# Idle transposes in the early gaps of a planned kernel, five places for raw weights, and a new order of its steps

## The chip, the cores and the metric

The kernel runs on one core of a Trainium2 chip. The metric is the device time of one execution in microseconds (us); lower is better. The engines are TensorE (PE for its matmuls, PEld for its weight loads), VectorE (DVE), ScalarE (ACT), GpSimd (POOL) and SyncE (SP, which here issues nearly all DMA transfers).

## What is computed

A banded attention with four sink keys feeds a gated MLP whose gate is a short convolution along the sequence. There are 4 batches, 8 heads, 768 positions and a head size of 64; the MLP is 512 wide with 1024 hidden units.

```python
scores = scale * np.matmul(q, k.transpose(0, 1, 3, 2))
keep = (pos[None, :] < n_sink) | ((rel >= 0) & (rel < window))     # n_sink 4, window 128
a = softmax(np.where(keep, scores, -1e9))
x = (a @ v) as (B, S, H * D)
h = np.maximum(x @ w_in, 0.0)
conv_out = sum(conv_w[k] * shifted(h, k) for k in range(3))
out = (h * sigmoid(conv_out)) @ w_out
```

The inputs q, k and v are 32-bit floats; `w_in`, `conv_w` and `w_out` come as 64-bit floats and are narrowed on the core.

## The kernel before

**Work.** The attention goes by pairs of heads (`g`, 16 of them, four in a batch) and by query tiles of 128 rows (`t`, six in a pair). For a tile, `scores` multiplies the queries with up to two tiles of keys, VectorE masks and takes the row maximum, ScalarE takes the exponential and its sum, GpSimd divides; `transp` transposes the probabilities on TensorE and GpSimd cuts them into two triangles; `pv` multiplies three tiles with v. Pairs 0 to 3 (batch 0) multiply in plain 32 bits, and their matmuls use 64 rows of the array (`narrow="rows"`); the later ones split each operand into a high and a low part. `pv` writes 64 columns of the array (`narrow=True`). The result goes to `x`, in two parts.

The MLP goes by units: 96 of them, each 128 hidden columns of 256 positions. A unit has twelve matmuls into one bank of PSUM (`ph`, line 791), a gate on ScalarE, VectorE and GpSimd, and twice three matmuls into the accumulators `po` (line 827). The units of a batch can begin when its four pairs have written `x`.

**Weights.** Seventeen pieces of raw weights (eight of `w_in`, eight of `w_out`, the taps) are read by SP at line 718 into places in `room[1]`, the space that later holds `x` of batch 1. There are three places. ScalarE and VectorE narrow each piece (lines 650 and 728 to 731), ScalarE rounds the high part, and GpSimd (for `w_in`) or VectorE (for `w_out`, line 744) takes the low part. A place is free when the narrowing has read it. `room[0]` holds a stretch of zeros in its first 792 columns.

**Order.** The kernel's order is not that of the program's loops. Every step is declared with an engine, an assumed duration, what it reads and writes, and a priority `at`, made from the numbers in `LAY`. `Plan.run` walks through time: for each engine it takes, among the steps whose inputs are ready (or will be within `SLACK`), the one of the lowest priority; a buffer is a `Place` with a number of slots (`PLACES`), and a step waits for a slot. TensorE's steps are assumed to take twice as long while the plan holds its clock to be low. The order that comes out is what is issued, engine by engine; on the chip each engine then works through its list in order. Two `po` banks are lent to the scores until these have taken `LENT` (36) slots, two for a tile.

**Start and end.** Before the branch on `n_sink` and `window`, TensorE does 13, 3 and 4 transposes of the identity into an unused tile (line 1271 and 1275), with the first transposes of q and k between them; the first halves of q and k are loaded by SP (line 345). At the end the two last output tiles are copied out of PSUM, the first by ScalarE with its store on ScalarE's queue, the second whole by VectorE (line 833) with its store on SP's.

Of the kernel before, what the change touches and what calls it, by code (L numbers as in the profile page):

```python
# [17 lines left out]
P = 128  # L18
# [10 lines left out]
RAWB = 4  # L29
# [310 lines left out]
def load(c, g, nm, t, lo, hi):  # L340

    b, hp = divmod(g, c.H // 2)
    for j in range(2):
        src = getattr(c, nm)[b, 2 * hp + j].rearrange("(t p) d -> p t d", p=P)
        c.nc.sync.dma_start(t[:, :, j, :], src[:, lo:hi])
    return t


def load_half(c, g, nm, half, slot):
    n = c.S // P // 2  # L350
    return load(c, g, nm, slot, n * half, n * half + n)
# [10 lines left out]
SLACK = {"PE": 0, "ACT": 0, "DVE": 21, "POOL": 451, "SP": 0}  # L362
SWITCH = 95
WINDOW, SHIFT = 3413.0, 0.0
# [3 lines left out]
CONV, GATED, PICK, WIL = "sbuf", False, 0, "POOL"  # L368
CARE = 112.0
LENT = 36  # L370
# [63 lines left out]
class Plan:  # L434
# [39 lines left out]
    def run(self):  # L474
        free = dict.fromkeys(("PE", "ACT", "DVE", "POOL", "SP"), 0.0)
        slow, window, used, kind = True, SHIFT, 0.0, None
# [22 lines left out]
        while left:  # L499
# [13 lines left out]
            e = o.eng  # L513
            if e == "PE" and o.narrow != mode:
                t += SWITCH + (70 if mode else 0)
                mode = o.narrow
# [3 lines left out]
            if e == "PE":  # L520
                while t >= window + WINDOW:
                    slow = used < (0.97 if slow else 0.55) * WINDOW
                    window, used = window + WINDOW, 0.0
                if slow:
                    busy, late = 2.0 * busy, late + busy
                used += busy
# [25 lines left out]
            if o.size:  # L552
                fabric = max(t + o.busy, fabric) + o.size / 225.0
                o.end = fabric + 1150.0
# [20 lines left out]
        return order  # L575


class Banded:


    def __init__(self, c):
# [26 lines left out]
        self.raws = [self.room[1][:, 1024 * i:1024 * i + 1024] for i in range(3)]  # L608
        self.zero = self.nc.gpsimd.to_reg(0.0)
        self.tiles = 0  # L610

# [51 lines left out]
    def dma(self, size, fn, r, w, n=1, busy=500, **kw):  # L663
        return self.p.op("SP", busy * n, busy * n, fn, r, w, size=size, **kw)
# [3 lines left out]
    def setup(self):  # L668
        c, nc, p = self.c, self.nc, self.p
        p.at = -9.0  # L670
        p.op("DVE", 1900, 1900, lambda: None, (), ("before", "tri", "m0", "m1", "m2"))
        p.op("POOL", 200, 200, lambda: None, (), ("vs",))
        p.at = LAY["zeros"]
        self.pool(760, lambda: nc.gpsimd.memset(self.zeros, 0.0), ("room",), ("zeros",), port=False)
# [36 lines left out]
    def weight(self, name, src, at, taps=None, parts=None, spot=None, engine=None, early=1.5):  # L711
# [6 lines left out]
        self.dma(rows * n * (8 if wide else 4), lambda: nc.sync.dma_start(dst() if not wide else dst().bitcast(I32), src if not wide else src.bitcast(I32)), ("room",), (raw,), busy=410)  # L718
        p.at = at
        if wide:  # L720
            low = self.turn("st", [P, 512], F32, f"{name}l")
            w = self.turn("st" if CONV == "sbuf" else "h", [P, 512], F32, f"{name}w")
# [3 lines left out]
            two = CONV == "sbuf"  # L726
            self.act(lv, lambda: f(words(1)), n + 60, (raw, "room"), (low,), scale=2.0 ** -112, sbuf=True)
            self.dve(n, lambda: nc.vector.tensor_scalar(wint(), lint(), 3, None, ALU.logical_shift_left), (low,), (w,), fast=two, port=two)
            self.dve(n, lambda: nc.vector.scalar_tensor_tensor(out=wint(), in0=words(0), scalar=29, in1=wint(), op0=ALU.logical_shift_right, op1=ALU.bitwise_or), (raw, w, "room"), (w,), port=two)
            v, vv = (low, lv) if not two and (taps is not None or engine == "POOL") else (w, wv)  # L730
            self.dve(n, lambda: nc.vector.scalar_tensor_tensor(out=vv().bitcast(I32), in0=lint(), scalar=-0x80000000, in1=wint(), op0=ALU.bitwise_and, op1=ALU.bitwise_or), (low, w), (v,), port=two)
            w, wv = v, vv
# [9 lines left out]
        psum = wide and CONV != "sbuf" and engine != "POOL"  # L742
        self.act(lambda: H, wv, n, (w,), ((name, "H"),), sbuf=not psum)
# [493 lines left out]
def attention_gated_mlp(ctx: ExitStack, tc: tile.TileContext, q, k, v, n_sink, window, w_in, conv_w, w_out, out):  # L1237
# [7 lines left out]
    with tc.manual_schedule():  # L1245
# [14 lines left out]
        for i in range(2):  # L1260
            load_half(c, 0, "qk"[i], 0, c.raw[i])
# [86 lines left out]
```

## Time and profile before

| what | us |
| --- | --- |
| median of 3 runs | 469.26 |
| lowest and highest | 467.88, 469.94 |
| the profiled execution's own time | 469.77 |
| its span, first to last instruction | 468.0 |
| TensorE busy in the span | 444.2 |
| VectorE, ScalarE, GpSimd busy | 358.2, 323.6, 295.8 |

The profile is one execution. The time around the span is 1.77 us. "Busy" of TensorE counts from the start of a matmul to its modelled end, so neighbouring matmuls overlap. The granted clock is a share of full speed. In a list of waits, the engine and line that waited stand first, then what ended the wait, the sum in us, the number and the longest. In a timeline a row is a run of like instructions: its start, its length, the engine, line, operation, output and inputs, the number, and in brackets the idle time before it.

### The profile page before, as it was taken

Reading aid. Unit: us, or ns where it says so; the run is one execution under the profiler, and the core shown is the slowest. Engines: PE = TensorE matmul, PEld = TensorE weight load, DVE = VectorE, ACT = ScalarE, POOL = GpSimd, SP = SyncE. Lnnn points to the kernel's source line nnn. Section 1 sums busy time; section 2 is a strip of 40 time slices with the busy share of each in tenths; the row PEclk is TensorE's granted clock in tenths of the full one; section 3 lists DMA queues with packets and bytes.
Section 4 is the critical chain, followed back from the end, with each engine's and each line's share of the span. In section 5 each row is a group of like instructions: output and inputs, shape, how many; then the busy total and the mean of one; then the engine's idle time right before and its main releaser. Section 6 shows DMA issues by size and latency. Waiting matters only on the chain.

```text
span 468.0 us, 10388 instructions
## 1 busy us (share of the span) xinstructions
PE 444.2 (95%) x3097; PEld 377.4 (81%) x3097; DVE 358.2 (77%) x1260; ACT 323.6 (69%) x1054; POOL 295.8 (63%) x587
## 2 busy tenths in 40 slices
PE   7678879999999999999999999999999999999995
PEld 6445657778888887988898988888898888999883
DVE  6788999999889987796777787697876764555552
ACT  3998877878788887775777786686775753545451
POOL 3698787767867777646565776657577672444442
PEclk9999989999999999999999999999999999999999
DMA  6797797415252433060513224160210010101011
GB/s 149 208 245 185 217 265 198 93 33 128 75 114 49 112 107 80 18 147 24 131 52 86 53 75 109 23 166 1 56 61 0 9 40 0 46 1 47 1 46 53
DMA packets 87306, 41.01 MB, mean 88 GB/s; under 512 B 80160, under 2 KB 80184, under 8 KB 87240
## 3 DMA queue, kind: packets, MB, share of 16 engines
q1 hardware_dynamic: 86952, 39.99, 33.5%
q8 instruction: 27, 0.44, 0.4%
q14 instruction: 39, 0.32, 0.2%
q10 hardware_dynamic: 288, 0.26, 0.2%
HBM read 27.60 MB, written 6.29 MB: 72 GB/s over the span
## 4 chain that ended last, share of the span: by engine, by line
PE 81%; DMA 8%; DVE 4%; ACT 3%; issue 1%; POOL 1%; SPq 1%; ACTq 0%; DVEq 0%
PE ph L791 29%; PE po L827 28%; PE px L1080 7%; DMA roomL<-in_moe_w_in_dram 4%; PE sc L983 4%; PE pts L1022 4%; PE sc L984 3%; PE tk L910 2%; PE tq L932 2%; PE px L1088 1%; DMA raw<-in_k_dram 1%; ACT pe L995 1%; DMA sc_i<-in_window_dram 1%; DMA roomL<-in_moe_conv_w_dram 1%; DMA vsr<-roomH 1%
## 5 line engine op out<-in xcount | busy, mean ns | idle before, releaser
L827 PE MATMUL po<-woH,g 128*128 128x512 f32 x384 | 149.0, 405 | 0.0
L1001 POOL TENSOR_SCALAR pe<-pe,sm 128x132 f32<-128x132 f32 (+1 forms) x192 | 90.1, 480 | 52.5 <-DVE sm L999 35.4
L791 PE MATMUL ph<-xH,wiL 128*128 128x258 f32 (+1 forms) x384 | 111.1, 293 | 0.0
L791 PE MATMUL ph<-xH,wiH 128*128 128x258 f32 (+1 forms) x384 | 109.2, 288 | 0.9 <-DVE kk L916 0.5
L791 PE MATMUL ph<-xL,wiH 128*128 128x258 f32 (+1 forms) x384 | 109.4, 289 | 0.0
L995 ACT ACTIVATE pe<-pe,sm 128x132 f32<-128x132 f32 (+1 forms) x192 | 76.9, 402 | 19.9 <-DVE sm L990 19.3
L816 POOL TENSOR_SCALAR g<-t 128x256 fp32r<-128x256 f32 x96 | 43.1, 449 | 63.6 <-DVE t L815 42.9
L827 PEld LDWEIGHTS po<-woH,g 128*128 128x128 f32 x384 | 72.4, 189 | 10.2
L817 POOL TENSOR_TENSOR g<-t,g 128x256 fp32r<-128x256 f32 x96 | 76.2, 794 | 6.8
L791 PEld LDWEIGHTS ph<-xL,wiH 128*128 128x128 f32 x384 | 72.1, 189 | 5.7 <-issue 2.6
L791 PEld LDWEIGHTS ph<-xH,wiH 128*128 128x128 f32 x384 | 72.1, 189 | 5.5 <-ACT pe L995 0.9
L827 PE MATMUL po<-woL,g 128*128 128x512 f32 x192 | 75.8, 395 | 0.0
L791 PEld LDWEIGHTS ph<-xH,wiL 128*128 128x128 f32 x384 | 72.2, 190 | 4.1 <-issue 2.5
L812 DVE SCALAR_TENSOR_TENSOR t<-hb,cw,t 128x256 f32<-128x256 f32 x96 | 53.5, 558 | 25.8 <-ACT t L650 25.6
L815 DVE SCALAR_TENSOR_TENSOR t<-t,hb 128x256 f32<-128x256 f32 x96 | 44.3, 465 | 24.9 <-ACT t L646 24.5
L646 ACT ACTIVATE t<-t 128x256 f32<-128x256 f32 x96 | 40.0, 420 | 32.2 <-DVE t L813 31.8
L1032 POOL TENSOR_SCALAR_AFFINE_SELECT pT<-pT 128x256 f32<-128x256 f32 x80 | 38.2, 478 | 32.8 <-ACT pT L648 28.4
L646 ACT ACTIVATE hb<-ph 128x258 f32<-128x258 f32 (+1 forms) x96 | 36.9, 385 | 29.4 <-PE ph L791 27.4
L650 ACT ACTIVATE t<-hb,cw 128x256 f32<-128x256 f32 x96 | 49.0, 512 | 11.2 <-POOL g L817 8.0
L813 DVE SCALAR_TENSOR_TENSOR t<-hb,cw,t 128x256 f32<-128x256 f32 x96 | 52.6, 549 | 1.9
L990 DVE CUSTOM_DVE_ANT_0 pe<-sc,m 128x132 f32<-128x132 f32 (+1 forms) x192 | 51.0, 287 | 4.0 <-PE sc L984 2.4
L989 DVE COPY_PREDICATED sc<-before,sc 128x128 f32<-128x128 int32 x160 | 43.0, 289 | 12.7 <-PE sc L984 10.1
(182 smaller groups left out, 860.6 us busy)
## 6 DMA issues: line engine op xcount, KB each, us to landing
raw<-in_q_dram SPq DMA_DIRECT2D x64, 96.0 KB
raw<-in_k_dram SPq DMA_DIRECT2D x64, 96.0 KB
out_dram<-out SPq DMA_DIRECT2D x23, 256.0 KB
kk<-kk SPq DMA_DIRECT2D x24, 198.0 KB
vraw<-in_v_dram SPq DMA_DIRECT2D x24, 192.0 KB
roomL<-in_moe_w_in_dram SPq DMA_DIRECT2D x8, 512.0 KB
roomL<-in_moe_w_out_dram SPq DMA_DIRECT2D x8, 512.0 KB
vraw<-in_v_dram SPq DMA_DIRECT2D x8, 128.0 KB
```

Of the source, the lines that this page charges most:

```text
L646: nc.scalar.activation(o, i, func, **({} if scale is None else {"scale": scale}))
L650: nc.scalar.mul(o, i, scale() if callable(scale) else scale)
L791: nc.tensor.matmul(h.ap[:, 0:W], self.wi[i][:, cc, ff * P:(ff + 1) * P], x[k][:, cc, t0:t1], start=(q == 0), stop=(q == len(prods) - 1))
L812: self.dve(324, lambda: stt(out=uv(), in0=this(), scalar=cw(1), in1=yv(), op0=ALU.mult, op1=ALU.add), (hb, y), (u,), port=not gated)
L813: self.dve(324, lambda: stt(out=yv(), in0=nxt(), scalar=cw(2), in1=uv(), op0=ALU.mult, op1=ALU.add), (hb, u), (y,), port=not gated)
L815: self.dve(256, lambda: stt(out=a.ap, in0=uv(), scalar=1.0, in1=this(), op0=ALU.add, op1=ALU.mult), (u, hb), (a,), port=not gated)
L816: self.pool(355, lambda: nc.gpsimd.tensor_scalar(g.ap[:, 0], a.ap, 1.0, 1.0, ALU.mult, ALU.mult), (a,), ((g, 0),))
L817: self.pool(685, lambda: nc.gpsimd.tensor_tensor(out=g.ap[:, 1], in0=a.ap, in1=f(g.ap[:, 0]), op=ALU.subtract), (a, (g, 0)), ((g, 1),), po ...
L827: nc.tensor.matmul(po.ap[:, 0:c.DM], g.ap[:, k, tt * P:(tt + 1) * P], w[:, ff, :], start=(ff == 0 and i == 0), stop=(ff == NFF - 1 and i = ...
L990: self.dve(n + 14, lambda pc=pc, j=j: nc.vector.tensor_tensor_reduce(out=pe()[:, j, cols], in0=pc.ap[:, P:SW][:, cols], in1=mk, op0=ALU.ad ...
L995: p.op("ACT", 395, 505, lambda j=j: nc.scalar.activation(pe()[:, j, cols], pe()[:, j, cols], AF.Exp, bias=sm[:, j:j + 1], scale=-1.0, accu ...
L1001: work = (lambda e, j=j: e.tensor_scalar(pe()[:, j, cols], pe()[:, j, cols], sm[:, 8 + j:9 + j], 1.0, ALU.mult, ALU.mult), ((smk, 8), (pt, ...
```

## The change

- **Idle transposes.** When the plan takes a TensorE step before `WARM` (75 us of plan time) that also takes a PSUM bank (`h`, `sc`, `pts` or `px`), and TensorE would stand idle before it, the plan puts `n` transposes of the identity in front, into that bank: as many as fill `FILL` (0.9) of the gap at 110 ns each. They wait for the bank to be released, as the step does.
- **Places.** Raw weights get five places instead of three; the two new ones are columns 1024 to 3071 of `room[0]`. The raw halves of q and k get five instead of four (`RAWB`).
- **Plan.** The model of a changing clock goes; assumed rates of transfers by kind, `LAND`, `ROWS`, `SLACK`, `CARE` and nearly all priorities in `LAY` are new; `LENT` is 48 instead of 36.
- **Start.** The first half of k is loaded from ScalarE's queue. The mask `tri` is no longer made (nothing used it). The zeros of `room[0]` have another priority and follow the masks.
- **End.** The next to last output tile is stored by SP; the last one is copied in two halves at once, by VectorE and by ScalarE, each with its own store, on SP's and ScalarE's queue (`close`).
- Options that were off (`GATED`, `PICK`, `CONV`, `WIL`) are taken out without an effect.

```diff
-RAWB = 4
+RAWB = 5
...
-SLACK = {"PE": 0, "ACT": 0, "DVE": 21, "POOL": 451, "SP": 0}
+SLACK = {"PE": 8.038, "ACT": 12.964, "DVE": 7.163, "POOL": 475.892, "SP": 0}
...
+RATE = {"w": 310.0, "v": 212.0, "in": 240.0, "out": 370.0}
+LAND = 1300.0
+ROWS = 45
+CARE = 83.141
+FILL, WARM = 0.9, 75000.0
+LENT = 48
...
+            if e == "PE" and not (mode and o.narrow) and t < WARM:
+                out = SWITCH + 70 + (ROWS if mode == "rows" else 0) if mode else 0
+                n, x = self.idle(o, free[e] + out, t)
+                if n > 0:
+                    y = self.warm(x, n)
+                    y.start, mode = max(free[e] + out, y.ready), False
+                    y.end = free[e] = y.start + y.busy
+                    order.append(y)
+                    t, kind = max(t, free[e]), y.fn.__code__
...
+    def idle(self, o, at, t):
+        for x in o.turns:
+            if x.slot is None and x.place.kind in ("h", "sc", "pts", "px"):
+                return int(FILL * (t - max(at, x.place.free[0][0] + 200.0)) / 110.0), x
+        return 0, None
+
+    def warm(self, x, n):
+        o = Op()
+        o.eng, o.busy, o.late, o.size, o.narrow, o.what, o.port = "PE", 109.0 * n, 109.0 * n + 165, 0, False, "warm", False
+        o.fn = lambda: [self.idler(x.ap) for i in range(n)]
...
-        self.raws = [self.room[1][:, 1024 * i:1024 * i + 1024] for i in range(3)]
+        self.raws = [self.room[1][:, 1024 * i:1024 * i + 1024] for i in range(3)] + [self.room[0][:, 1024 * i:1024 * i + 1024] for i in (1, 2)]
...
+        def idler(ap):
+            while len(ap.shape) > 2:
+                ap = ap[:, 0]
+            c.nc.tensor.transpose(ap[:, 0:P], c.ident, c.ident)
...
+    def close(self, b, rows, po, st):
+        c, nc = self.c, self.nc
+        w = c.DM // 2
+        for x in range(2):
+            cols = slice(w * x, w * x + w)
+            if x:
+                self.act(lambda cols=cols: st.ap[:, cols], lambda cols=cols: po.ap[:, cols], w, (po,), ((st, x),))
+            else:
+                self.dve(w, lambda cols=cols: nc.vector.tensor_copy(st.ap[:, cols], po.ap[:, cols]), (po,), ((st, x),))
+            q = nc.scalar if x else nc.sync
+            self.dma(131072, lambda cols=cols, q=q: q.dma_start(c.out[b, rows, cols], st.ap[:, cols]), ((st, x),), (("out", "close", x),), rate="out", busy=100)
...
-LAY = {"w0": 3.68, "w": 1.53, "early": 5.65, "load": 9.74, "v": -7.75, "prep": 4.7, "span": -0.89, "load2": -16.22, "v2": -4.52,
+LAY = {"w0": 1.33, "w": 1.58, "early": 5.33, "load": 11.46, "v": -0.58, "prep": 4.99, "span": -4.35, "load2": -2.65, "v2": 5.8,
...
-PLACES = {"h": 2, "po": 2, "sc": 2, "px": 1, "pts": 1, "raww": 3, "st": 3, "hb": 2, "t1": 2, "t2": 2, "g": 6, "raw": RAWB, "vraw": 2,
+PLACES = {"h": 2, "po": 2, "sc": 2, "px": 1, "pts": 1, "raww": 5, "st": 3, "hb": 2, "t1": 2, "t2": 2, "g": 6, "raw": RAWB, "vraw": 2,
...
-            load_half(c, 0, "qk"[i], 0, c.raw[i])
+            load_half(c, 0, "qk"[i], 0, c.raw[i], (nc.sync, nc.scalar)[i])
...
-        m.tri = con.tile([P, P], F32, name="tri")
-        nc.vector.tensor_scalar(m.tri, R, 0.0, None, ALU.is_gt)
```

## Rows read from the trace of the kernel before

**Rows 1.** The page: busy time of each engine, and the granted clock in 40 slices.
```profile
PE 444.2 (95%) x3097; PEld 377.4 (81%) x3097; DVE 358.2 (77%) x1260; ACT 323.6 (69%) x1054; POOL 295.8 (63%) x587
...
PEclk9999989999999999999999999999999999999999
```
**Rows 2.** Busy time by stretches: length, each engine, granted clock, DMA share, GB/s.
```profile
9.00:72.00 63.00, 49.83 (x348) 33.37 (x348) 55.10 (x224) 53.37 (x184) 49.85 (x85) 0.97 0.87 225
72.00:100.00 28.00, 26.39 (x184) 21.41 (x184) 27.55 (x95) 21.52 (x71) 18.44 (x36) 1.00 0.49 121
100.00:455.00 355.00, 354.50 (x2508) 311.49 (x2509) 267.11 (x919) 243.87 (x791) 221.35 (x442) 1.00 0.24 61
455.00:468.00 13.00, 7.37 (x35) 5.78 (x33) 2.92 (x6) 2.32 (x5) 2.59 (x4) 0.99 0.14 48
```
**Rows 3.** The same view for parts of the first 100 us.
```profile
9.00:44.00 35.00, 27.25 (x190) 16.90 (x191) 28.04 (x144) 30.24 (x113) 26.80 (x51) 1.00 0.83 215
44.00:100.00 56.00, 48.97 (x343) 37.88 (x341) 54.62 (x175) 44.65 (x142) 41.50 (x70) 0.97 0.70 179
...
36.00:40.00 4.00, 3.14 (x24) 2.04 (x24) 3.16 (x18) 3.37 (x16) 3.12 (x8) 1.00 0.20 65
40.00:72.00 32.00, 26.35 (x186) 18.68 (x185) 30.45 (x93) 27.13 (x82) 26.85 (x43) 0.95 0.93 242
56.00:58.00 2.00, 1.72 (x14) 1.22 (x10) 2.00 (x10) 1.31 (x4) 1.93 (x4) 1.00 0.94 237
```
**Rows 4.** Waits of TensorE from 9 to 72 us.
```profile
PE pts L1022 <- ACT pT L648: 3.6, 3, 2.2
...
PE tk L1045 <- ACT kp L648: 0.2, 1, 0.2
```
**Rows 5.** Waits of SP's queue from 30 to 60 us.
```profile
SPq L718 <- DVE wi_0w L729: 2.4, 1, 2.4
SPq L718 <- DMA roomL<-in_moe_conv_w_dram: 2.2, 1, 2.2
SPq L718 <- DVE tapsw L729: 1.3, 1, 1.3
```
**Rows 6.** Timeline of SP's queue from 33 us.
```profile
33.41 0.90 SPq L345 DMA_DIRECT2D vraw<-in_v_dram  x2
37.93 0.35 SPq L718 DMA_DIRECT2D roomL<-in_moe_w_out_dram  x1
```
**Rows 7.** Busy time by stretches around the drop of the clock.
```profile
61.50:64.80 3.30, 3.01 (x15) 1.92 (x17) 3.30 (x13) 2.87 (x10) 2.82 (x6) 0.50 0.99 255
```
**Rows 8.** Timeline of TensorE: the same steps at two clocks.
```profile
8.96 1.55 PE L975 MATMUL sc<-t,pT 64*128 64x128 f32 x8
...
28.34 0.93 PE L975 MATMUL sc<-kp,X 64*128 64x128 f32 x8
...
52.65 1.52 PE L1080 MATMUL px<-pT,vraw 128*64 128x128 f32 x16
...
59.05 0.55 PE L910 MATMUL tk<-ident,raw 128*128 128x128 f32 x3 [0.49 <-ACT sT L648]
...
61.79 0.90 PE L910 MATMUL tk<-ident,raw 128*128 128x128 f32 x3 [1.19 <-ACT hb L646]
62.62 2.62 PE L1080 MATMUL px<-pT,vraw 128*64 128x128 f32 x16
```
**Rows 9.** The chain that ended last, around the first `po` work.
```profile
72.66 0.71 PE po L827 x3
...
79.55 0.70 PE po L827 x3
```
**Rows 10.** Timeline of VectorE before the branch.
```profile
1.74 1.68 DVE L1285 TENSOR_SCALAR tri<-vraw 128x128 f32<-128x128 f32 x1
...
5.06 0.17 DVE L66 CAST sc_f<-sc_i 128x4 f32<-128x4 int32 x1 [1.51 <-DMA sc_i<-in_window_dram]
```
**Rows 11.** Timeline of the end.
```profile
461.72 0.59 ACT L648 COPY out<-po 128x512 f32<-128x512 f32 x1 [3.35 <-PE po L827]
...
462.41 0.69 DVE L833 COPY out<-po 128x512 f32<-128x512 f32 x1 [3.58 <-PE po L827]
463.13 0.33 SPq L837 DMA_DIRECT2D out_dram<-out  x1
```

More of the change, by code (lines that the diff above doesn't have):

```diff
@@ L475, in run @@
         free = dict.fromkeys(("PE", "ACT", "DVE", "POOL", "SP"), 0.0)
-        slow, window, used, kind = True, SHIFT, 0.0, None
+        kind = None
         ready = {e: [] for e in free}
@@ L552, in run @@
             if o.size:
-                fabric = max(t + o.busy, fabric) + o.size / 225.0
-                o.end = fabric + 1150.0
+                fabric = max(t + o.busy, fabric) + o.size
+                o.end = fabric + LAND
             for x in o.turns:
@@ L575, in run @@
         return order
+    def idle(self, o, at, t):
[7 more added lines that the diff above has]
+        o.fn = lambda: [self.idler(x.ap) for i in range(n)]
+        o.at, o.n, o.deps, o.soft, o.outs, o.turns, o.need, o.tag = (0.0, 0), len(self.ops), set(), set(), [], [x], 0, "warm"
+        at, x.slot, was = x.place.take()
+        o.ready, o.before = at, [] if was is None else [was]
+        self.ops.append(o)
+        return o
 class Banded:
@@ L717, in weight @@
         dst = lambda: raw.ap[0:rows, 0:n * (2 if wide else 1)]
[L718 removed]
+        self.dma(rows * n * (8 if wide else 4), lambda: nc.sync.dma_start(dst() if not wide else dst().bitcast(I32), src if not wide else src.bitcast(I32)), ("room",), (raw,), busy=410, rate="w")
         p.at = at
@@ L725, in weight @@
             wint, lint = (lambda: wv().bitcast(I32)), (lambda: lv().bitcast(I32))
-            two = CONV == "sbuf"
             self.act(lv, lambda: f(words(1)), n + 60, (raw, "room"), (low,), scale=2.0 ** -112, sbuf=True)
[L728 to L732, printed above, removed]
+            self.dve(n, lambda: nc.vector.tensor_scalar(wint(), lint(), 3, None, ALU.logical_shift_left), (low,), (w,), fast=True, port=True)
+            self.dve(n, lambda: nc.vector.scalar_tensor_tensor(out=wint(), in0=words(0), scalar=29, in1=wint(), op0=ALU.logical_shift_right, op1=ALU.bitwise_or), (raw, w, "room"), (w,), port=True)
+            self.dve(n, lambda: nc.vector.scalar_tensor_tensor(out=wint(), in0=lint(), scalar=-0x80000000, in1=wint(), op0=ALU.bitwise_and, op1=ALU.bitwise_or), (low, w), (w,), port=True)
         else:
@@ L758, in weights @@
             for cc in range(self.NCC):
-                self.weight(f"wi{half}_{cc}", vi[:, cc, s], ats[n], parts=self.wi, spot=(slice(None), cc, s), engine=WIL, early=LAY["early"])
+                self.weight(f"wi{half}_{cc}", vi[:, cc, s], ats[n], parts=self.wi, spot=(slice(None), cc, s), engine="POOL", early=LAY["early"])
                 n += 1
@@ L976, in scores @@
             p.at = at if t % 2 == 0 else at - 1 + LAY["two"]
-            self.pe(1.7 * w + 10, both, (X, *((kk, g, x) for x in halves), (kk, g, "s")), pcs, narrow="rows", what=f"sc{g}_{t}").plain = plain
+            self.pe(1.65 * w + 9, both, (X, *((kk, g, x) for x in halves), (kk, g, "s")), pcs, narrow="rows", what=f"sc{g}_{t}").plain = plain
             p.at = at
```

80 lines of the change are left out of this document (29 added, 51 removed), and 6 rows, old and new, of the table LAY.

## The prediction, written before the result was known

> **What bounds the kernel now.** I read the page first, then a table of busy time by stretches, then the waits of TensorE and of SP's queue, and last the timelines of single places. The page says that TensorE is busy for 95% of the span [rows 1]. A share over the whole span hides where the rest lies, so the stretches come next [rows 2]. From 100 to 455 us TensorE is busy for 354.50 of 355.00 us at full clock: there nothing but less TensorE work could save time, and the change takes none away. From 9 to 72 us it is idle for 63.00 - 49.83 = 13.17 us, from 72 to 100 us for 1.61 us, and after 455 us for 5.63 us, mostly the last copies and stores. TensorE's work is the same in both kernels, so the end moves by what the idle time of the first 100 us changes, plus what the low clock takes, plus the tail.
>
> In the early stretch no engine alone is full. The DMA engines are at 0.87 over 9 to 72 us and at 0.93 over 40 to 72 us [rows 2, 3]; VectorE is at 28.04 of 35.00 us up to 44 us, with 6.96 us free, and then at 54.62 of 56.00 us up to 100 us [rows 3]. So after 44 us VectorE is nearly full, and what makes it so is partly weight narrowing that could have been done earlier if the weights had been there. TensorE's waits in the stretch are many and short: ten groups, from 3.6 us for ScalarE's copies of `pT` down to 0.2 us [rows 4]. They are the ends of chains through the other engines, so no single wait is the one to remove. The queue that feeds them is SP's: it works in order, and when it stands at line 718 for a free weight place, the loads of q, k and v behind it stand too.
>
> **The change part by part.**
>
> *Five weight places.* SP waits at line 718 for 2.2 + 1.3 us and for 2.4 us [rows 5]. The first is one stop: the load of v ends its issue at 33.41 + 0.90 = 34.31 us and the next weight is issued at 37.93 us, 3.6 us later [rows 6]. What was waited for is the place that the taps held, until they had landed and VectorE had read them. Behind it the DMA engines ran dry: their share from 36 to 40 us is 0.20, against 0.93 in the 32 us that follow [rows 3]. The transfer time lost is 4.00 x (0.93 - 0.20) / 0.93 = 3.1 us, and since the engines are nearly full afterwards, everything that landed later was late by about as much. With five places the load finds a place and the stop goes. The second stop (2.4 us) cost nothing: from 56 to 58 us the share stayed at 0.94, since enough was queued. So this part gives between 0 and 3.1 us; I take 3.1, because the row after the stop shows full DMA engines, and because VectorE's 6.96 free us before 44 us can take the earlier narrowing. The fifth place for raw q and k acts in the same direction and is not added.
>
> *New priorities.* They add and remove no instruction. They can move TensorE's 13.17 us of idle time either way: the bound on a gain is all of it, the bound on a loss I take from the idle transposes below. Weights come earlier (`w0` from 3.68 to 1.33), and with them VectorE's work, in the direction of the first part; I add nothing of its own. In the full stretch after 100 us there are 0.50 us of idle time to win [rows 2].
>
> *Idle transposes.* They stand on TensorE directly in front of a step that waits for the same PSUM bank; behind them in the list is that step and everything after it. If the gap is there, the wait for data hides them and they cost nothing. If it isn't, they cost 0.9 of the planned gap: with gaps like those of the kernel before, at most 0.9 x 13.17 = 11.9 us. I take 0 as they are made for 0.9 of a gap, and keep 11.9 as the far end. What they can give back is the low clock. It was granted at 0.50, the lower of the two levels (1.2 GHz), for 3.30 us from 61.50 us [rows 7], after a stretch with several idle gaps, the last of 1.19 us [rows 8]. There 16 matmuls with v took 2.62 us against 1.52 us at the upper level, and three transposes 0.90 against 0.55 us [rows 8]: 1.10 + 0.35 = 1.45 us. Between 0 and 1.45 us, I take 1.4. The first ten us are slow too, though the rows give no lower clock for them: eight score matmuls at 8.96 us took 1.55 us, and eight like them at 28.34 us 0.93 us [rows 8]. Before the branch the counts of idle transposes don't change, so this stays.
>
> Up to that first rise TensorE had done mainly transposes, but score matmuls too, so the trace doesn't say whether transposes alone hold the clock. The Trainium skill, "TensorE: Matmul & The Clock Gate", section on PE-mode transpose (Part 4), says that a transpose does not count as TensorE activity in the way a matmul does, and that the full clock doesn't engage for it. By that rule the idle transposes would give nothing of the 1.45 us. That is a rival below.
>
> *`LENT` 48.* The `po` banks now come back only after the scores of all 24 tiles of batch 0. In the kernel before, just one half of a unit's `po` work ran before the last such scores, at 72.66 us, and the next at 79.55 us [rows 9]. Between 0 and 0.71 us is pushed back; I take 0.4 lost.
>
> *Start.* Making `tri` took 1.68 us, but VectorE then stood idle until the transfer of `n_sink` and `window` had landed [rows 10], so that is 0 (the cover is that transfer; without it, up to 1.68 us). The load of k from ScalarE's queue frees SP earlier, but the branch depends on the same transfer: 0.
>
> *End.* The last tile is copied by VectorE in 0.69 us and then issued in 0.33 us; ScalarE copies a whole tile in 0.59 us and is done at 462.31 us, before VectorE starts its copy at 462.41 us [rows 11]. Two halves at once take between half of 0.59 and 0.59 us, and end 0.1 to 0.4 us sooner; the stores of half the size can land sooner as well, for which there is no row (0 to 0.4). I take 0.4 in all, between 0.1 and 0.8. If the halves did not overlap, it would be nothing.
>
> **Sum.** 3.1 + 1.4 - 0.4 + 0.4 = 4.5 us. The profiled execution took 469.77 us (its span of 468.0 and 1.77 us around it), which is 0.5 us above the median of 469.26; it would become 465.3 us, and the median 464.8 us.
>
> **Rivals.**
>
> *The feed was not the limit* (the transfer was hidden): TensorE's early waits end with ScalarE and GpSimd more often than with a transfer [rows 4], and VectorE is full from 44 us on [rows 3]. Then the 3.1 us fall away: 1.4 us gained, 467.9 us. Against it stands the dry stretch of the DMA engines.
>
> *Transposes don't hold the clock.* As a mechanism of this kernel: between gaps filled with identity transposes the clock falls as before, and the 1.4 us stay lost: 3.1 us gained, 466.2 us. For it speaks that the first ten us were slow through a row of transposes; against it, that the rise came when most of the work just before was transposes.
>
> *More is won.* Stop, order and places together let VectorE use its 6.96 free us before 44 us. Then 7.0 us take the place of 3.1: 8.4 us gained, 460.9 us. For it: VectorE's full stretch begins just there. Against: GpSimd and ScalarE are not free at the same time (26.80 and 30.24 of 35.00 us).
>
> *Idle transposes hold up real work* (the other side). They are in an in-order list by the plan's clock, not the chip's. Where TensorE comes later to a gap than planned, the gap is gone but its transposes are still there. They cost 11.9 us at the most; at 4.5 / 11.9 = 38% of them in the way the gain is used up, and from 6.9 / 11.9 = 58% on the kernel is slower by more than 0.5%. At 60%: 7.1 us lost against 4.5 won, 471.9 us. For it: the early waits are short and of many kinds, so the plan can't know them well. Against: 10% of each gap is left over, and the step waits for data anyway.
>
> **How the numbers follow.** No change that can be told is within 0.5%, 466.9 to 471.6 us. Chances: the forecast (462.5 to 466.5 us) 0.42; more is won 0.17; transposes don't hold the clock 0.10; the feed was not the limit 0.18; idle transposes in the way 0.13. Faster by over 0.5% are the first two and 0.07 of the third, 0.66; within 0.5% the rest of the third and the fourth, 0.21; slower 0.13. The time predicted is 464.8 us. The range is 460.0 to 470.5 us: it takes in the second case at its worked time, the whole of the third and fourth, and part of the last; about 0.08 stays out below and 0.10 above.
>
> **What would show it.** Right: no stop of SP at line 718 beyond a few tenths of a us, no DMA slice as low as 0.20 between 9 and 70 us, VectorE's busy time before 44 us up by 3 us or more, TensorE's first full stretch beginning some 3 us before 72 us, no granted clock of 0.50 after 10 us, and a last copy of some 0.3 us on two engines. Transposes of the identity would stand in the gaps with real steps following on data. Wrong: idle transposes that end after the data of the step behind them have come; TensorE full only from 72 us or later; more idle time in TensorE between 100 and 455 us; or a lower clock in spite of the transposes.

## The result and the profile after

| | median us | lowest to highest | executions |
| --- | --- | --- | --- |
| before | 469.15 | 467.88 to 471.24 | 10 |
| after | 472.02 | 470.19 to 473.18 | 10 |

The ratio after to before is 1.0053, with a 95% interval of 1.0028 to 1.0078. The changed kernel is some 2.5 us slower, where 4.5 us were to be gained. Its profiled execution took 473.0 us with a span of 471.3 us, 3.3 us more of span than before. Four single executions among all runs took 613 to 855 us, with the core in a slower state, and are left out of every ratio and clock below.

The page after, first the busy time of each engine, then the granted clock in 40 slices, against [rows 1] (a digit of PEclk is the granted share of full speed in tenths):

```profile
PE 452.4 (96%) x3173; PEld 386.6 (82%) x3173; DVE 359.8 (76%) x1259; ACT 324.9 (69%) x1055; POOL 292.7 (62%) x587
...
PEclk9998999999999999999999999999999999999999
```

TensorE has 76 instructions more, the idle transposes, and is busy for 8.2 us more. Busy time by stretches, with the columns of [rows 2] and [rows 3]:

```profile
9.00:72.00 63.00, 56.50 (x406) 40.51 (x404) 55.94 (x228) 51.79 (x183) 48.01 (x80) 0.97 0.85 230
72.00:100.00 28.00, 26.62 (x198) 22.85 (x194) 27.09 (x90) 22.66 (x74) 22.03 (x38) 1.00 0.39 91
100.00:455.00 355.00, 353.51 (x2502) 309.77 (x2502) 267.01 (x917) 244.57 (x791) 214.91 (x442) 1.00 0.25 63
...
9.00:44.00 35.00, 30.41 (x204) 21.16 (x202) 28.75 (x135) 27.91 (x105) 24.07 (x43) 0.95 0.90 245
44.00:100.00 56.00, 52.72 (x399) 42.19 (x397) 54.28 (x183) 46.54 (x152) 45.97 (x76) 1.00 0.58 151
36.00:40.00 4.00, 4.00 (x20) 2.09 (x19) 3.97 (x18) 2.90 (x11) 3.31 (x7) 0.57 1.11 276
```

The feed did what was foreseen: the DMA share from 36 to 40 us is 1.11, which is full (0.20 before), and up to 44 us 0.90 (0.83). But VectorE's busy time up to 44 us, which should have grown by 3 us or more, grew by 0.7 us. TensorE is busy for 6.67 us more from 9 to 72 us. A group of 14 transposes takes 1.69 us, 0.109 us for each further one (each is 0.273 us long and they overlap); 62 of the 76 stand in this stretch, 6.8 us. So it does no more real work there than before: 406 - 62 = 344 matmuls against 348. After 100 us it is idle for 1.49 us instead of 0.50. In this profile the low clock lies between 36 and 40 us (0.57), before at 61.5 us.

Of SP's waits one longer stop for a weight place is left, 2.1 us, now for VectorE (columns: us in total, times, longest):

```profile
SPq L747 <- DVE wi_1w L757: 2.1, 1, 2.1
```

TensorE's timeline after, the start, the drop of the clock, a group of transposes and the first `po` work:

```profile
6.48 0.88 PE L1300 MATMUL preq<-ident,raw 128*128 128x128 f32 x3 [2.02 <-DMA raw<-in_q_dram]
...
9.64 1.67 PE L1006 MATMUL sc<-t,pT 64*128 64x128 f32 x8
...
34.38 0.41 PE L1053 MATMUL pts<-ident,pe 128*128 128x128 f32 x2 [1.39 <-POOL wiL L769]
...
37.56 2.34 PE L1107 MATMUL px<-pT,vraw 128*64 128x128 f32 x12
...
75.52 1.69 PE L638 MATMUL sc<-ident 128*128 128x128 f32 x14
...
78.88 0.44 PE L846 MATMUL po<-woH,g 128*128 128x512 f32 x1
```

The first scores come at 9.64 us, against 8.96 us [rows 8]: q is waited for until 6.48 us. The drop follows a gap of 1.39 us that holds no transposes.

Thirteen groups of transposes come after 10 us, and behind twelve of them TensorE's next real step starts without idle time. For one of them, GpSimd's copy that the step needs, the transposes, and the step:

```profile
67.52 0.74 POOL L1061 TENSOR_SCALAR_AFFINE_SELECT pT<-pT 128x256 f32<-128x256 f32 x1
...
68.25 0.82 PE L638 MATMUL px<-ident 128*128 128x128 f32 x6
69.00 1.30 PE L1107 MATMUL px<-pT,vraw 128*64 128x128 f32 x12
```

The data were there at 68.26 us, the step began at 69.00 us: these six were in the way for 0.7 us. That is the sign that the prediction named for its rival, transposes that end after the data of the step behind them have come. Its other signs of being wrong are there too: TensorE is not full before 72 us, it is idle for longer after 100 us, and the clock falls in spite of the transposes. And the timeline of the end, against [rows 11]:

```profile
464.55 1.06 ACT L677 COPY out<-po 128x512 f32<-128x512 f32 x2 [3.35 <-PE po L846]
...
465.64 0.42 DVE L867 COPY out<-po 128x256 f32<-128x256 f32 x1 [3.98 <-ACT out L677]
466.09 0.33 SPq L869 DMA_DIRECT2D out_dram<-out  x1
```

ScalarE's entry is its whole tile and its half of the last one, merged, and ends at 465.61 us. Only then does VectorE copy its half, and its idle time ends with ScalarE's copy: the halves don't overlap.

### The profile page after: what moved, and what is told of

Read it like the earlier page. It is cut to its first block, busy times and chain, and to the rows that moved or that the text cites. A ratio compares the mean times of both kernels' runs of the same rounds, so it can differ in the third digit from the quotient of the medians.

```text
span 471.3 us, 10505 instructions
## 1 busy us (share of the span) xinstructions
PE 452.4 (96%) x3173; PEld 386.6 (82%) x3173; DVE 359.8 (76%) x1259; ACT 324.9 (69%) x1055; POOL 292.7 (62%) x587
## 4 chain that ended last, share of the span: by engine, by line
PE 77%; DVE 10%; POOL 4%; ACT 3%; DMA 2%; issue 2%; SPq 0%; ACTq 0%; POOLq 0%; DVEq 0%
PE po L846 27%; PE ph L816 26%; PE px L1107 7%; PE pts L1053 3%; PE sc L1014 3%; PE sc L1015 3%; PE tq L963 2%; POOL pe L1032 2%; PE tk L941 2%; DMA raw<-in_q_dram 2%; PE px L1115 1%; DVE pe L1021 1%; DVE sc L1020 1%; DMA kk<-kk 1%; PE sc L1006 1%
## 5 line engine op out<-in xcount | busy, mean ns | idle before, releaser
L1032 POOL TENSOR_SCALAR pe<-pe,sm 128x132 f32<-128x132 f32 (+1 forms) x192 | 85.0, 454 | 43.4 <-DVE sm L1030 28.2
L816 PE MATMUL ph<-xH,wiL 128*128 128x258 f32 (+1 forms) x384 | 109.4, 289 | 0.0
L831 DVE SCALAR_TENSOR_TENSOR t<-hb,cw,t 128x256 f32<-128x256 f32 x96 | 54.5, 569 | 28.0 <-ACT t L679 27.4
L834 DVE SCALAR_TENSOR_TENSOR t<-t,hb 128x256 f32<-128x256 f32 x96 | 45.9, 479 | 25.1 <-ACT t L675 24.6
L1021 DVE CUSTOM_DVE_ANT_0 pe<-sc,m 128x132 f32<-128x132 f32 (+1 forms) x192 | 52.1, 287 | 4.2 <-PE sc L1015 1.4
L832 DVE SCALAR_TENSOR_TENSOR t<-hb,cw,t 128x256 f32<-128x256 f32 x96 | 52.9, 552 | 1.5
```

The lines of the kernel that those rows point to most:

```text
L816: nc.tensor.matmul(h.ap[:, 0:W], self.wi[i][:, cc, ff * P:(ff + 1) * P], x[k][:, cc, t0:t1], start=(q == 0), stop=(q == len(prods) - 1))
L831: self.dve(324, lambda: stt(out=e.ap, in0=this(), scalar=cw(1), in1=a.ap, op0=ALU.mult, op1=ALU.add), (hb, a), (e,), port=True)
L832: self.dve(324, lambda: stt(out=a.ap, in0=nxt(), scalar=cw(2), in1=e.ap, op0=ALU.mult, op1=ALU.add), (hb, e), (a,), port=True)
L834: self.dve(256, lambda: stt(out=a.ap, in0=e.ap, scalar=1.0, in1=this(), op0=ALU.add, op1=ALU.mult), (e, hb), (a,), port=True)
L1021: self.dve(n + 14, lambda pc=pc, j=j: nc.vector.tensor_tensor_reduce(out=pe()[:, j, cols], in0=pc.ap[:, P:SW][:, cols], in1=mk, op0=ALU.ad ...
L1032: work = (lambda e, j=j: e.tensor_scalar(pe()[:, j, cols], pe()[:, j, cols], sm[:, 8 + j:9 + j], 1.0, ALU.mult, ALU.mult), ((smk, 8), (pt, ...
```

## The experiments

My theory after the result: TensorE did not lack what the feed brought, and the small edits and the new order cost. The rivals: the transposes stand in the way; weights put ahead of the attention hold it up (theory A in some of the expectations; B is that of the transposes in the way). Every ratio below is to the kernel before, run beside it on the same chip in five rounds, with its 95% interval; 0.1% is 0.47 us.

### Was the feed worth anything?

**Five places, the plan made anew** by before's priorities.

```diff
-PLACES = {... "raww": 3, ...
+PLACES = {... "raww": 5, ...
```

> The kernel before with five places for raw weights and nothing else of the change; its plan is made anew with them. My prediction's step (the stop of SP for a weight place is worth 3.1 us): 466 us against 469.2. Theory A (the transfers were not the limit, the engines are): within 1 us of the kernel before, or slower where earlier weights come in front of attention.

Measured 1.0125 (1.0099 to 1.0151), 5.9 us slower. Its stretches:

```profile
9.00:44.00 35.00, 27.05 (x183) 17.07 (x183) 30.37 (x141) 31.08 (x115) 27.99 (x49) 0.95 0.97 267
...
72.00:100.00 28.00, 23.74 (x172) 20.02 (x171) 27.11 (x70) 20.70 (x63) 17.51 (x29) 0.98 0.29 68
```

The DMA engines are fuller up to 44 us than in either kernel (0.97), VectorE too; TensorE is not (27.05 us, 27.25 before [rows 3]). After 72 us it has 4.26 us of idle time, 2.65 more than before [rows 2]. More places change what is ready when, and with that the whole order.

**Five places, before's order kept**: the plan runs with three places, and the program uses five in turn.

```diff
-        raw = self.stand("raww", self.raws)
+        raw = Turn(self.place["raww"], lambda i: self.next_raw())   # next of five tiles
```

> The kernel before with five places for raw weights, used in turn, while every engine keeps the order of the kernel before (a plan made anew with five places took 474.8 us). Only the stop of SP for a free place can go. My prediction's step, taken alone: DMA share from 36 to 40 us near 0.9 and 3.1 us gained, 465.7 us. Theory A (what the transfers bring earlier waits for VectorE, GpSimd and ScalarE, which are the limit): the DMA share rises as well, but the time stays within 1 us of the kernel before, 468 to 469.5 us.

Measured 1.0002 (0.9979 to 1.0025). Its stretches, then SP's longest wait for a weight place and a longer one for a place of v:

```profile
36.00:40.00 4.00, 3.43 (x27) 2.35 (x27) 3.66 (x20) 3.68 (x17) 3.93 (x9) 1.00 0.57 176
...
9.00:44.00 35.00, 30.11 (x185) 18.49 (x186) 27.66 (x143) 30.69 (x115) 27.41 (x52) 0.85 0.87 226
```
```profile
SPq L345 <- PE px L1085: 2.6, 2, 2.2
...
SPq L719 <- ACT xH L649: 1.4, 2, 1.1
```

The stop of [rows 6] is gone, though SP now stops for 2.2 us a little later, for the place of a v that TensorE has to read first. The dry stretch is at 0.57 instead of 0.20, and the time is the same: the interval (a gain of 1.0 us to a loss of 1.2 us) leaves no room for 3.1 us. The clock was lower in this profile up to 44 us (0.85), which could hide a gain; but with idle transposes added, at mean clocks of 0.987 to 0.997, the same places measure 1.0008 (below). The feed was not the limit.

### Do the transposes hold the clock, and at what price?

**No transposes**, order and all else as in the changed kernel; **twice as many** in each group. Transposes are no part of the computation.

```diff
-        o.fn = lambda: [self.idler(x.ap) for i in range(n)]
+        o.fn = lambda: None                                        # none
+        o.fn = lambda: [self.idler(x.ap) for i in range(2 * n)]    # twice
```

> The changed kernel with its 76 planned idle transposes left out; every other instruction on every engine stands in the same order. Theory A (the order of the steps is what is slow: the narrowing of weights stands in front of batch 0's attention on GpSimd, VectorE and ScalarE, and the transposes only fill time that is idle anyway): within 1 us of the changed kernel, 471 to 473 us. Theory B (the transposes stand in the way of real steps): at least 2 us of their 8.3 us (76 x 0.109) come back, 470 us or less. Theory C (the transposes do hold the clock, and without them it falls oftener): 473 us or more and a lower mean clock.

> The changed kernel with each planned group of idle transposes twice as long, the order otherwise the same. Theory A: the second half of each group no longer fits a gap, so some of the further 8.3 us is added, 2 to 6 us, 474 to 478 us, and the first half is still free. Theory B: each transpose costs about the same, so what the first 76 cost comes once more. Theory C: the granted clock does not fall any more after 12 us, which gives back 1.5 to 1.8 us of it.

None: 1.0054 (1.0032 to 1.0076), as slow as with them. Twice: 1.0106 (1.0076 to 1.0137). The mean granted clock of the executions was 0.992 to 0.999 with the transposes, 0.980 to 0.988 without, 0.993 to 0.999 with twice as many. The stretch from 9 to 72 us, without and then with twice as many:

```profile
9.00:72.00 63.00, 54.78 (x357) 36.74 (x354) 56.30 (x237) 54.24 (x189) 51.13 (x83) 0.90 0.88 238
```
```profile
9.00:72.00 63.00, 59.74 (x468) 45.17 (x466) 57.71 (x232) 52.35 (x185) 48.45 (x80) 1.00 0.86 229
```

So they hold the clock, 0.90 to 0.97 to 1.00 in this stretch. The first helping makes no difference to the time (0.0%, -0.3 to 0.3), the second costs 0.5% (0.1 to 0.9). The first is a net figure: some transposes are in the way, as seen above, and the clock gives something back; the pair doesn't tell the two apart.

**Before's order with 55 transposes** put into its own gaps (as many as fill twice the gap that the plan expects), and the same **with the five places in turn**:

```diff
+            if e == "PE" and t < 75000.0 and not (mode and o.narrow):
+                n = int(2.0 * (t - max(free[e] + out, x.place.free[0][0])) / 110.0)
+                o.fn = ([self.idler(x.ap) for i in range(n)], fn())   # x: the step's bank of PSUM
```

> The kernel before with 55 idle transposes put in front of TensorE steps for which its plan expects a gap before 75 us, order unchanged. If transposes hold the clock and cost little where TensorE waits anyway: mean clock 0.995 or more in all executions, against 0.976 to 0.997 seen for the kernel before, and 0.5 to 1.5 us gained, 467.5 to 468.3 us. If transposes don't count for the clock: mean clock as before and 0 to 2 us lost. If they stand in the way by their full length (55 x 0.109): 3 us or more lost and a high clock.

> Before's order with the five places used in turn and the idle transposes, without the change's start and end. If the start and end alone carry the loss found with before's order (all but the order: ratio 1.0034), this one is within 0.1 percent of before; if the transposes carry it, it is at before +1.0 us or more.

Measured 1.0026 (1.0002 to 1.0051) and 1.0008 (0.9983 to 1.0033). The mean clocks were 0.987 to 0.997 in both, 0.976 to 0.997 (0.988 on average) in the 106 executions of the kernel before that ran beside the experiments: higher, though not at 0.995 or more in every execution, as was expected of the first. The 1.4 us of the low clock don't come back with either. The first one's profile has a clock of 1.00 from 9 to 72 us, and the 16 matmuls with v that took 2.62 us in [rows 8] take 1.52 us, but behind 15 transposes:

```profile
61.31 1.80 PE L623 MATMUL px<-ident 128*128 128x128 f32 x15
63.05 1.52 PE L1094 MATMUL px<-pT,vraw 128*64 128x128 f32 x16
```

**The changed kernel without transposes, start and end**, to be set beside the one with transposes (start and end undone, below, 1.0041):

> The changed kernel with start and end undone and without the planned transposes: new order and five places alone. If the transposes give as much by the clock as they take by standing in front: 470.2 to 471.2 us, as with them (470.7), and a mean clock below 0.990. If they cost more than they give: 469.7 us or less.

Measured 1.0072 (1.0047 to 1.0097), clocks of 0.983 to 0.984 instead of 0.993 to 0.999: here taking the transposes away costs 0.3% (0.0 to 0.6), in the pair above nothing (-0.3 to 0.3); the two can't be told apart. A last pair runs **before's order inside the changed kernel** (each engine takes only the head of a list written down from the plan of before; start and end undone, `LENT` 36), with 46 transposes (its expectation says 69; the page counts 3143 matmuls against 3097) and without:

```diff
-                found = [(t, o) for o in mine if (t := when(o)) is not None]
+                found = [(t, o) for o in mine if o is self.queue[e][0] and (t := when(o)) is not None]
```

> The changed kernel with start and end undone and the order of the kernel before throughout; five places, the transposes in the gaps that the new assumptions show, and no mask tri remain of the change. If the order is the whole of the loss that is left: the time of the kernel before within 0.7 us, 468.4 to 469.8 us. If places or transposes cost by themselves: 470 us or more.

> The run with before's order in the changed kernel, now without its 69 transposes, so that TensorE has fewer instructions. That run's profile ended 7.7 us after TensorE's last matmul instead of 5.7, with one fetch of instructions more behind the last store. If that tail is what made it slow and it hangs on the count of instructions, the fetch is gone here, the tail is 5.7 us and the time is before -0.5 to +1.5 us. If the tail has another cause, or the cost lies elsewhere, the time stays at before +2.5 us or more.

Measured 1.0066 (1.0044 to 1.0087) and 1.0113 (1.0083 to 1.0143). Stretches with the transposes, two steps of scores, and TensorE's last matmul:

```profile
9.00:44.00 35.00, 30.62 (x214) 20.51 (x214) 28.20 (x146) 31.24 (x118) 28.17 (x53) 0.95 0.93 237
...
9.00:72.00 63.00, 54.87 (x389) 39.77 (x388) 55.20 (x231) 54.10 (x186) 51.58 (x88) 0.95 0.91 236
72.00:80.00 8.00, 8.00 (x60) 6.20 (x60) 7.02 (x27) 5.54 (x19) 5.67 (x11) 1.00 0.39 104
```
```profile
43.87 1.15 PE L1008 MATMUL sc<-kp,X 64*128 64x260 f32 x8
...
74.92 0.71 PE L1008 MATMUL sc<-kp,X 64*128 64x260 f32 x4
...
461.28 0.39 PE L847 MATMUL po<-woH,g 128*128 128x512 f32 x1
```

and without:

```profile
9.00:44.00 35.00, 28.12 (x199) 17.64 (x199) 28.80 (x146) 31.19 (x118) 28.02 (x53) 1.00 0.92 237
...
9.00:72.00 63.00, 50.64 (x350) 34.62 (x351) 55.78 (x231) 54.26 (x186) 51.47 (x88) 0.97 0.90 235
72.00:80.00 8.00, 8.00 (x53) 6.08 (x53) 5.59 (x19) 5.05 (x18) 4.42 (x7) 0.83 0.39 97
```
```profile
43.92 1.15 PE L1008 MATMUL sc<-kp,X 64*128 64x260 f32 x8
...
76.33 0.71 PE L1008 MATMUL sc<-kp,X 64*128 64x260 f32 x4
...
462.86 0.39 PE L847 MATMUL po<-woH,g 128*128 128x512 f32 x1
```

The first has the lower clock up to 44 us (0.95 against 1.00), and yet the same step comes at 43.87 and 43.92 us: what that low clock took was made up in a stretch in which TensorE waits for others. From 72 us on TensorE is busy for 8.00 of 8.00 us, and nothing is made up: a clock of 0.83 there means 8.00 x 0.17 x 2 = 2.7 us at half speed, 1.4 us of work lost. The next pair of steps is 1.41 us apart, and the first run's last matmul comes 1.58 us sooner. These are two single executions. They show what a low clock costs in either place, not that the transposes decide where it falls.

### The start and the end

**Both undone in the changed kernel** (k on SP's queue, the last tile whole by VectorE), its order unchanged; **both done in the kernel before**; and each **alone in the kernel before**:

```diff
-            load_half(c, 0, "qk"[i], 0, c.raw[i], (nc.sync, nc.scalar)[i])
+            load_half(c, 0, "qk"[i], 0, c.raw[i], nc.sync)
-                    self.close(b, rows, po, st)
+                    self.dve(c.DM, lambda ...: nc.vector.tensor_copy(st.ap, po.ap[:, 0:c.DM]), (po,), (st,))
```

> The changed kernel with the first half of k loaded by SP again and the last tile copied whole by VectorE, as before the change; the plan's order is the same. If the start and the end are what the traces seem to show (first score matmul at 9.64 instead of 8.96 us; the half copies one after the other, so that the span ends 6.1 instead of 5.7 us after TensorE's last matmul): 0.7 + 0.4 = 1.1 us sooner, 470.9 us. If the start is hidden by what follows: 0.4 us, 471.6 us.

> The kernel before with only the start (k on ScalarE's queue) and the end (the last tile closed in halves by two engines) of the change. By the rows of the changed kernel the first score matmul comes 0.68 us later and the tail behind TensorE's last matmul is 0.4 us longer: +0.7 to +1.1 us if both reach the end. If the start is made up behind (the first 70 us are full of waits for loads), +0.4 us or nothing.

> The kernel before with k's first half on ScalarE's queue and nothing else. q landed 0.68 us later with it (wait of 2.02 us against 1.34). If that delay reaches the end, before +0.5 to +0.9 us; if the waits for loads behind it swallow it, within 0.3 us of before.

> The kernel before with the last tile closed in two halves by ScalarE and VectorE and nothing else. If the halves follow each other, as the rows of the changed kernel show (VectorE's at 465.64 us, after ScalarE's), and the store of the first half waits as the other does, before +0.3 to +1.0 us with TensorE's last matmul where it was; if they win what the smaller copy is shorter, before -0.4 us.

Measured: undone 1.0041 (1.0027 to 1.0056) against 1.0053 with both; done on before 1.0032 (1.0007 to 1.0058), k alone 1.0017 (0.9997 to 1.0036), halves alone 1.0020 (0.9994 to 1.0045). The two single edits sum to the pair, though each by itself reaches just short of being told from nothing. The start in the kernel before, then with k on ScalarE's queue:

```profile
5.80 0.87 PE L1273 MATMUL preq<-ident,raw 128*128 128x128 f32 x3 [1.34 <-DMA raw<-in_q_dram]
```
```profile
6.43 0.52 PE L1273 MATMUL preq<-ident,raw 128*128 128x128 f32 x3 [1.97 <-DMA raw<-in_q_dram]
...
8.22 0.93 PE L975 MATMUL sc<-t,pT 64*128 64x128 f32 x8 [0.18 <-ACT t L1277]
```

The end with halves, then whole (k alone), both in the kernel before:

```profile
463.04 0.39 PE L827 MATMUL po<-woH,g 128*128 128x512 f32 x1
...
463.87 0.42 DVE L848 COPY out<-po 128x256 f32<-128x256 f32 x1 [3.98 <-ACT out L648]
464.32 0.33 SPq L850 DMA_DIRECT2D out_dram<-out  x1
```
```profile
460.55 0.39 PE L827 MATMUL po<-woH,g 128*128 128x512 f32 x1
...
461.70 0.33 SPq L837 DMA_DIRECT2D out_dram<-out  x1
```

q is waited for until 6.4 instead of 5.8 us in this kernel too. In that execution the first scores came sooner all the same, at 8.22 instead of 8.96 us [rows 8], since they ran at the upper level of the clock already (eight in 0.93 instead of 1.55 us). With halves the last issue comes 1.28 us after the start of TensorE's last matmul, with the whole copy 1.15 us after it. The halves win nothing and put one store more behind.

### The order

**All of the change but the order**, in the kernel before: five places in turn, transposes, start and end, by the edits above (`LENT`, the fifth place for raw q and k and `tri` stay as before).

> The kernel before, its order of work kept, with the rest of the change: the five places used in turn, idle transposes, k on ScalarE's queue, the last tile closed in halves. If the order is what costs (single edits to before's order so far: places +0.0 us, transposes +1.2 us by the ratio 1.0026), this run comes out at before +0.5 to +2.0 us, at least 1 us under the changed kernel's +2.9. If the parts themselves cost what the change cost, whatever the order, it comes out at +2.5 us or more.

Measured 1.0034 (1.0013 to 1.0056): 1.6 of the 2.5 us (0.6 to 2.6) are there with before's order; start and end alone measured 1.5.

**Later weights**, and **the later attention's priorities of before**, each in the changed kernel with start and end undone:

```diff
-LAY = {"w0": 1.33, ...
+LAY = {"w0": 3.68, ...                      # later weights
+LAY = {"load2", "v2", "prep2", "span2", "tr", "pv", "soft", "xs", "sink": as before}
```

> The changed kernel with start and end undone and the weights' first priority as before the change (3.68 instead of 1.33), so that narrowing comes later against the attention of batch 0. Theory A (narrowing in front of attention is what makes the new order slow): at least 1 us sooner than without this edit (470.7 us), 469.7 us or less, and TensorE further on at 50 us. Theory D: no gain, 470.3 to 471.5 us.

> The changed kernel with start and end undone and, besides, the priorities of the attention after batch 0 (loads, preparation, transposes, products with v, softmax, sinks) as before the change; the early priorities, places and transposes are the new ones. Theory D (the new order gains about 1 us up to 100 us and loses about 1.6 us between 290 and 400 us to the later order): 1 to 1.6 us sooner than without this edit (470.7 us), 469.1 to 469.7 us. Theory A alone (the loss is in the early stretch): 470.3 to 471 us.

Measured 1.0134 (1.0101 to 1.0166) and 1.0067 (1.0041 to 1.0093), against 1.0041 of the kernel they start from. The gain of 1 us that theory A expects of later weights is not there. Each of the two edits also makes the whole order anew, so neither says what one priority is worth.

**The new order up to 265 us of the plan, then before's; and the other way round** (lists as above):

> The changed kernel with start and end undone; its order is kept for the steps that its plan starts before 265 us, and all later steps stand in the order of the kernel before. Theory D (the new order loses about 1.6 us of TensorE progress between 290 and 400 us and nothing before): 469 us, as the kernel before, 1.6 us sooner than with the new order throughout (470.7 us). Theory E (what is lost is lost in the first 100 us): 470.5 to 471 us.

> The converse: the order of the kernel before for the steps that its plan starts before 265 us, and the order of the changed kernel for the later ones; places and transposes as in the changed kernel (the po banks come back after 36 slots, as this order needs). Theory D: 470.5 us. Theory E: 469 us.

Measured 1.0047 (1.0026 to 1.0067) and 1.0122 (1.0094 to 1.0149). From 250 to 400 us, the changed kernel first, then before's order with the new one behind it:

```profile
250.00:400.00 150.00, 149.47 (x1067) 129.69 (x1066) 111.19 (x392) 102.83 (x333) 89.27 (x187) 1.00 0.20 51
```
```profile
250.00:400.00 150.00, 147.94 (x1053) 128.59 (x1051) 110.36 (x388) 103.17 (x334) 92.19 (x190) 1.00 0.20 52
```

TensorE stands for 0.53 and 2.06 us; with before's order throughout it is busy for 150.00 us. The new late order opens gaps where there were none, but before's late order behind the new start doesn't win them back (1.0047). No version beat the kernel before.

## Why the prediction was wrong

| step | predicted gain, us | measured, us | from |
| --- | --- | --- | --- |
| feed (five places) | 3.1 | -0.1 (-1.2 to 1.0) | places in turn, 1.0002 |
| clock (transposes) | 1.4 | 0.0 (-1.5 to 1.6), net of what they hold up | the changed kernel with and without, 1.0053 and 1.0054 |
| start and end | 0.4 | -1.5 (-2.7 to -0.3) | both on before, 1.0032 |
| order, `LENT`, the rest | -0.4 | -0.9 | 1.0053 less 1.0034 |

The interval of the last line, with those of its two ratios taken as independent, is -2.4 to 0.7 us: that the order costs anything of its own is not shown.

**The step that failed** is that of the five places: "since the engines are nearly full afterwards, everything that landed later was late by about as much", taken at 3.1 us. The stop and the dry DMA engines were real; with five places the stop goes and the dry stretch fills in good part, and the time stays where it was. Transfer time was counted as TensorE's time without following one late load to a step of TensorE that waited for it. The rows for that were there: VectorE is full from 44 us on [rows 3], and of the ten groups of waits in [rows 4], 12.9 us together, transfers ended two, 3.1 us:

```profile
PE trk L873 <- DMA raw<-in_k_dram: 2.0, 2, 1.4
...
PE px L1088 <- DMA vs<-in_v_dram: 1.1, 1, 1.1
```

The right case was the rival "the feed was not the limit", which had a chance of 0.18; its 467.9 us are wrong as well, by the other steps.

**The clock.** The mechanism held: transposes keep the clock up. The Trainium skill, "TensorE: Matmul & The Clock Gate", Part 4 (PE-mode transpose), says the opposite, that the full clock doesn't engage for transposes; by the clocks of 0.980 to 0.988 without and 0.992 to 0.999 with them, same order, it does not hold here. The size is not settled: by the pairs with and without, the transposes are worth 0.0 us (-1.5 to 1.6; changed kernel), 1.5 us (0.1 to 2.8; start and end undone), 2.2 us (0.5 to 3.9; before's order in the changed kernel), -1.2 us (-2.4 to -0.1; the kernel before) and -0.3 us (-1.9 to 1.3; the kernel before with five places). Two terms of the sum do not hold. The transposes were taken at no cost, since they fill 0.9 of a planned gap. And the 1.45 us, read off matmuls that ran slower at 61.5 us, were taken as paid in full, in a stretch where TensorE waits for others.

How much of a low clock is paid in the kernel before can be read off its own executions. Of the 106, the 15 with a mean clock of 0.981 or less (0.9779 on average) took 469.8 us on average, the 27 with 0.994 or more (0.9953) took 468.2 us. A TensorE that is never idle would have lost 0.0174 x 468 = 8.1 us between the two; 1.6 us, a fifth, shows in the time. These are differences between executions, not the effect of an edit. The profile that the prediction read had a clock of 0.996, among the highest: little was left to win in it.

**Transposes in the way**, the rival for "slower", had the right sign, and its mechanism is in the trace: steps whose data had come waited for transposes. But it is not the net cause of the loss, since removing all of them gives nothing (1.0054).

**The start.** It was put at 0 because "the branch depends on the same transfer". The transfer that counts is q's. Loading k from ScalarE's queue lets k start sooner, at 1.24 instead of 2.24 us, beside q; q came 0.68 us later in the changed kernel and 0.63 us later in the kernel before. How much of it reaches the end is not shown (k alone 1.0017, 0.9997 to 1.0036). The removal of `tri` was not tried by itself.

**The end.** "If the halves did not overlap, it would be nothing." They did not: the second copy starts only when the first has ended, and the last store is issued 0.13 us later than with a whole copy. Whether the chip or the program's own waits keep the two copies apart was not tried. The stores of half the size, for which no row was named, ended no sooner in any way that counts: the last data packet ended 3.75 us after the start of TensorE's last matmul before, 3.66 us after it in the changed kernel, 3.79 us with halves alone. No row of before showed two engines copying parts of one tile at once; a gain was taken for it all the same.

**`LENT`.** The first `po` work comes at 78.88 us, before at 72.66 us [rows 9]. TensorE had other work meanwhile; that this cost anything was not separated from the order.

**What stays open.** How much of the loss the order makes, and why before's order with the new one behind it (1.0122) is worse than either order by itself (1.0066 and 1.0041, start and end undone), while the other mixture (1.0047) lies between them. An order is a joint choice here: of the edits that changed it, every one came out between 0.4% and 1.3% slower than before. Open too is why before's order inside the changed kernel was at 1.0066 although TensorE ended on time in its profile; the tail, below, is there in that profile.

## What to carry to other kernels

A dry stretch of the DMA engines, or a stop of a queue, is worth time only if a load that it delays ends a wait of the engine that sets the end: follow one such load to its reader before its microseconds enter the sum. The same goes for a low clock: it costs its full half only where that engine is busy without a gap, and in this kernel a fifth of it showed. Work put into a gap needs a price too, for the gaps that come out shorter than planned. An edit at the end has nothing behind it that could cover it, so two engines sharing one tile need a row that shows them side by side before a gain is written down; so do two transfers at the start that now run at once.

## What the runs showed of the hardware

In two of the twenty profiles the span went on for 7.0 and 7.1 us behind the issue of the last store, in the others for 4.7 to 5.7 us. In the run with before's order and transposes in the changed kernel the last store is issued at 462.43 us and the span ends at 469.4 us, 7.0 us later; in the kernel before it is 4.9 us (463.13 to 468.0 us [rows 11]). What the DMA engines moved from 455 us on, in slices of 0.5 us, and the packets of the queues that fetch instructions:

```profile
GB/s 0 33 0 0 0 0 0 0 0 16 0 33 0 0 20 365 316 332 82 33 0 16 33 0 0 0 0 16 0 0 0 0 0 0 0 0 0 0 0 0
...
q14 instruction: 9, 0.07, 1.1%
```

and in the five places with before's order:

```profile
GB/s 0 0 0 0 0 0 0 0 0 16 33 0 0 16 209 307 373 197 37 8 0 16 16 16 0 0 0 0 0 0 0 0 0 0 0 0 0 0 0 0
...
q14 instruction: 8, 0.07, 1.0%
```

In both the stores (the slices of about 200 to 370) are over by 465 us and a few fetches follow; in the first one packet more comes at about 468.5 us, and the span ends behind it. Seven of the twenty profiles had this ninth packet. Before's order without transposes had it too, and 7.1 us; in the kernel with k alone on another queue it was there, and the 5.2 us behind its last issue are no more than the 4.7 to 5.3 us of the profiles without it. So the packet alone doesn't make the tail long. Nor does the count of instructions: the two long tails have 3143 and 3097 matmuls. What does was not found, and that the fetch holds the end up is not shown.
